# Gate products of a SwiGLU loop over 128 contraction rows in place of 96

## The chip, the cores and the metric

The kernel runs on one core of one Trainium2 chip. The metric is the device time of one execution in microseconds, the median of several runs. The five engines of the core are named PE (TensorE, matrix products), PEld (its loading of stationary operands), DVE (VectorE), ACT (ScalarE), POOL (GpSimd) and SP (SyncE, which here only issues transfers).

## What is computed

Three stages follow one another; the change touches the last.

```python
attn_out = _attn_ref(...)            # Fourier layer over 8 x 3072 tokens of width 256
x = attn_out.reshape(B * S, D)
x = _moe_ref(x=x, **moe_kwargs)      # ends in  c @ slot_out   (c: softmax over 32 slots)
# _moe2_ref:
g = x @ w_gate                       # 256 -> 1536
silu = g * (1.0 / (1.0 + np.exp(-g)))
val = x @ w_val
return (silu * val @ w_out)          # 1536 -> 256
```

Since x = c @ slot_out, the kernel computes slot_out @ w_gate and slot_out @ w_val once (32 x 1536 each, called the gates below) and then, for every token, c times these 32 rows.

## The kernel before

The first 600 us of the program are the Fourier layer, the logits, and the softmax statistics over all 24,576 tokens. The change lies behind that, in the function after_slots, which computes the 32 slot outputs and then runs the loop.

Numbers are held as a high part and a low part in a type (F32R) that TensorE multiplies in one pass. The softmax c of each token block stands in DRAM in the scratch array c_scr, index 0 the high part and index 1 the low part. A product of two split numbers is written as one matrix product whose contraction rows are blocks of 32: the stationary tile gst holds gate blocks, the moving tile cst holds softmax blocks, and row block r of the one meets row block r of the other. Before the change there are three blocks, so 96 rows: high x high, high x low, low x high.

- gates(t) computes a third of the gates into PSUM (tile pq), 64 rows for each of gate and value, in which the 32 slots stand twice. gate_high(c, m) copies 64 rows to gst rows 0 to 63 (the high part twice); gate_low(c, m) writes PSUM minus high part. There are eight such pairs (four column pieces c, two matrices m). They run ahead of and during the first steps of the loop.
- load_c(b, q) fills one cst tile by transfers that POOL's queue issues, one per block of 32 rows and 128 KB each. There are 24 tiles (8 batches b, 3 pieces q); a tag has two buffers.
- The loop has 576 steps (8 batches x 3 pieces x 2 halves x 12 column blocks of the gates). In a step gv(i) issues two gate products, L1561 into pg and L1562 into pv, with 512 moving columns. ACT forms sg = silu(pg) (L1564), DVE forms h = sg * pv (L1566). Then split(i-1) makes hh on ACT (L1573) and hl on DVE (L1574), and mm_out(i-3) issues six products with 128 rows (L1586) into the output accumulators o. So a step has eight products of TensorE, two of which have 96 rows.
- rest_c(b+1) interleaves the making of the next batch's softmax with the steps of batch b. POOL multiplies (L1622) and subtracts (L1636), SP stores both parts to c_scr, and then POOL's queue issues the transfers of the three load_c of the next batch (written at steps 50, 54 and 58 of the batch), and the load of the batch after that (L1612).

Order on an engine is the order in which the code is written. Each transfer of POOL's queue takes the next of eight semaphores in a ring, shown below as DMASW0 to DMASW7, and waits for the transfer that had this semaphore before it.

Of the kernel before, what the change touches and what calls it, by code (L numbers as in the profile page):

```python
# [10 lines left out]
F32 = mybir.dt.float32  # L11
F32R = mybir.dt.float32r
# [10 lines left out]
R1 = 96  # L23
# [340 lines left out]
def kernel(  # L364
# [49 lines left out]
    def open_pool(name, side="left", bufs=1, **k):  # L414
        cm = tc.tile_pool(name=name, bufs=bufs, reuse_waits="tile", **({} if "space" in k else {"side": side}), **k)
        pool = cm.__enter__()
        open_pools[name] = cm
        return pool
# [990 lines left out]
    def after_slots(ypool, chp):  # L1409
# [17 lines left out]
        for k in range(2):  # L1427
            nc.tensor.matmul(
                out=pst[:, k], lhsT=acc[:, k * 128:(k + 1) * 128], rhs=fd[:, 0:32], start=True, stop=True
# [51 lines left out]
        wp = open_pool("wp")  # L1481
        wp.tile([128, 312], F32, name="pad0", bufs=1)
        cp = open_pool("p2c", bufs=2)
        cuts = ((0, 0, 128), (0, 128, 512), (1, 0, 512), (2, 0, 512))
        gst = {(c, m): wp.tile([R1, cuts[c][2] - cuts[c][1]], F32R, name=f"gst{c}{m}") for c in range(4) for m in range(2)}

        def gate_cols(m, f):
            c, k = ((0, 0), (1, f - 1), (2, f - 4), (3, f - 8))[(f > 0) + (f > 3) + (f > 7)]
# [11 lines left out]
        cst_t = {}  # L1500

        def load_c(b, q):
            cst_t[b, q] = t = cp.tile([R1, 1024], F32R, tag=f"cst{q}", name="cst")
            for r, s in ((0, 0), (1, 1), (2, 0)):
                nc.gpsimd.dma_start(out=t[32 * r:32 * r + 32], in_=c_scr[b, s, 32 * q:32 * q + 32])

        load_c(0, 0)
        load_wo(wp, 0)
        load_wg(wp, "wg", 1, 2)
# [15 lines left out]
        ps = open_pool("p2ps", bufs=2, space=PSUM)  # L1525
        load_wo(hp, 1)
        load_c(0, 1)
        load_wo(hp, 2)
        load_c(0, 2)

        pq = {}
# [14 lines left out]
        def gate_low(c, m):  # L1546
            t, a, e = cuts[c]
            nc.vector.tensor_sub(  # L1548
                out=gst[c, m][64:96], in0=pq[t][64 * m:64 * m + 32, a:e], in1=gst[c, m][0:32].bitcast(F32)
            )  # L1550

        h_t, hs_t, po_t, ob_t = {}, {}, {}, {}
# [101 lines left out]
        for i in range(n + 3):  # L1654
            b, at = divmod(i, per)
            if at == 0:
                jobs = rest_c(b + 1) if b + 1 < B else {}
            if i == 0:
                gates(0)
                gates(1)  # L1660
            for c, m in {
                0: ((0, 0), (0, 1), (1, 0), (1, 1)), 1: ((2, 0),), 2: ((2, 1),), 4: ((3, 0),), 5: ((3, 1),),
            }.get(i, ()):
                gate_high(c, m)
                gate_low(c, m)
            if i < n:
                gv(i)
            if i == 1:
                gates(2)
            if 1 <= i <= n:  # L1670
                split(i - 1)
            for job in jobs.get(at, ()):
                job()
            if i >= 3:
                mm_out(i - 3)
        hp.tile([128, 504], F32, name="pad1", bufs=1)

    with tc.manual_schedule():
        after_slots(*phase1())
        for name in ("p2ps", "p2h", "p2c", "wp", "ypool", "chp"):  # L1680
            close_pool(name)
# [31 lines left out]
```

## Time and profile before

| | |
|---|---|
| median of 3 runs | 1684.48 us (1683.44 to 1685.2) |
| profiled execution, its own time | 1683.11 us |
| span of its trace | 1681.3 us |
| first gate product of the loop starts at | 604.76 us |
| PE busy | 1658.4 us (99%) |
| DVE busy | 1296.7 us (77%) |
| ACT busy | 981.4 us (58%) |
| POOL busy | 306.5 us (18%) |

The rows come from one profiled execution; times count from the start of its span. A matmul's record has a modelled end and overlaps the next one, so what a product costs in a dense stream is the distance between starts, not the duration shown.

### The profile page before, as it was taken

Reading aid. Unit: us, or ns where it says so; the run is one execution under the profiler, and the core shown is the slowest. Engines: PE = TensorE matmul, PEld = TensorE weight load, DVE = VectorE, ACT = ScalarE, POOL = GpSimd, SP = SyncE. Lnnn points to the kernel's source line nnn. Section 1 sums busy time; section 2 is a strip of 40 time slices with the busy share of each in tenths; the row PEclk is TensorE's granted clock in tenths of the full one; section 3 lists DMA queues with packets and bytes.
Section 4 is the critical chain, followed back from the end, with each engine's and each line's share of the span. In section 5 each row is a group of like instructions: output and inputs, shape, how many; then the busy total and the mean of one; then the engine's idle time right before and its main releaser. Section 6 shows DMA issues by size and latency. Waiting matters only on the chain.

```text
span 1681.3 us, 23324 instructions
## 1 busy us (share of the span) xinstructions
PE 1658.4 (99%) x8186; PEld 1282.1 (76%) x8186; DVE 1296.7 (77%) x2205; ACT 981.4 (58%) x1832; POOL 306.5 (18%) x353
## 2 busy tenths in 40 slices
PE   7999999999999999999999999999999999999998
PEld 4677676776767668888888888888888888888886
DVE  4789888888888558778778777778777777877776
ACT  2655565655656356656656656656655665665664
POOL 1334334334343421100100200200110110110000
PEclk9999999999999999999999999999999999999999
DMA  9356454546547971311300201311120031021111
GB/s 194 86 130 152 111 136 113 147 114 155 147 113 223 326 182 26 82 26 26 82 26 19 76 26 26 82 26 26 45 63 19 20 82 26 25 73 26 26 26 25
DMA packets 260164, 139.94 MB, mean 83 GB/s; under 512 B 210352, under 2 KB 243856, under 8 KB 260048
## 3 DMA queue, kind: packets, MB, share of 16 engines
q1 hardware_dynamic: 249648, 116.57, 26.7%
q0 software_dynamic: 9344, 21.63, 5.0%
q8 instruction: 65, 1.06, 0.3%
q14 instruction: 51, 0.42, 0.1%
q10 hardware_dynamic: 1056, 0.26, 0.1%
HBM read 72.74 MB, written 40.50 MB: 67 GB/s over the span
## 4 chain that ended last, share of the span: by engine, by line
PE 91%; DVE 3%; DMA 2%; ACT 1%; SPq 1%; issue 1%; POOL 0%; DVEq 0%; ACTq 0%; POOLq 0%
PE o L1586 47%; PE pb L701 10%; PE pv L1562 8%; PE pg L1561 8%; PE ac L587 6%; PE ac L613 4%; PE ch L1056 1%; PE ch L1104 1%; PE ch L798 1%; SPq L827 1%; PE ch L866 1%; DMA x<-in_x_dram 1%; PE ch L1012 1%; PE ch L926 1%; DVE xg L632 1%
## 5 line engine op out<-in xcount | busy, mean ns | idle before, releaser
L1586 PE MATMUL o<-hh,wo 128*128 128x512 f32 x2304 | 718.0, 393 | 0.0
L1564 ACT ACTIVATE sg<-pg 128x512 f32<-128x512 f32 x576 | 345.6, 600 | 410.7 <-PE pg L1561 410.6
L1566 DVE TENSOR_TENSOR h<-sg,pv 128x512 f32<-128x512 f32 x576 | 393.3, 683 | 245.3 <-ACT sg L1564 243.7
L1586 PEld LDWEIGHTS o<-hh,wo 128*128 128x128 f32 x2304 | 433.9, 188 | 104.3
L1586 PE MATMUL o<-hl,wo 128*128 128x512 f32 x1152 | 454.0, 394 | 0.0
L1574 DVE TENSOR_TENSOR hl<-h,hh 128x512 fp32r<-128x512 f32 x576 | 397.2, 690 | 0.1
L1573 ACT ACTIVATE hh<-h 128x512 fp32r<-128x512 f32 x576 | 358.9, 623 | 0.3 <-DVE h L1566 0.2
L1586 PEld LDWEIGHTS o<-hl,wo 128*128 128x128 f32 x1152 | 216.0, 188 | 47.1
L1562 PE MATMUL pv<-cst,gst 96*128 96x512 f32 x576 | 228.9, 397 | 0.6 <-DVE gst L1548 0.6
L1561 PE MATMUL pg<-cst,gst 96*128 96x512 f32 x576 | 227.5, 395 | 0.0
L701 PE MATMUL pb<-xg,whl 128*128 128x512 f32 x576 | 177.1, 437 | 0.3 <-DVE yt L756 0.2
L701 PEld LDWEIGHTS pb<-xg,whl 128*128 128x128 f32 x576 | 104.4, 189 | 44.2 <-issue 22.5
L1562 PEld LDWEIGHTS pv<-cst,gst 96*128 96x128 f32 x576 | 109.4, 190 | 25.8 <-DVE gst L1548 0.9
L1561 PEld LDWEIGHTS pg<-cst,gst 96*128 96x128 f32 x576 | 108.2, 188 | 25.4 <-DVE gst L1548 1.3
L772 POOL TENSOR_TENSOR yt<-r,yt 128x512 f32<-128x512 f32 x75 | 97.5, 1301 | 160.9 <-ACT yt L763 110.6
L592 DVE STREAM_TRANSPOSE chan<-ac 128x512 f32<-128x512 f32 x128 | 89.9, 707 | 37.3 <-PE ac L587 33.0
L1622 POOL TENSOR_TENSOR e<-e,rs 96x256 f32<-96x256 f32 x28 | 22.6, 835 | 502.4 <-DVE rs L1619 502.4
L587 PE MATMUL ac<-xq,fwd 96*128 96x512 f32 x224 | 111.6, 604 | 1.2 <-DVE xg L632 0.8
L613 PEld LDWEIGHTS ac<-cm,chan 128*128 128x128 f32 x768 | 101.0, 196 | 15.1 <-issue 6.6
L613 PE MATMUL ac<-cm,chan 128*128 128x128 f32 x768 | 105.0, 283 | 1.1 <-DVE xg L632 1.1
L701 PE MATMUL pb<-sg,whl 128*128 128x512 f32 x288 | 87.2, 426 | 0.3 <-POOL sg L651 0.3
L651 POOL TENSOR_TENSOR sg<-sf,sg 128x256 fp32r<-128x256 f32 x75 | 56.5, 758 | 119.5 <-ACT sg L647 104.1
(157 smaller groups left out, 1459.3 us busy)
## 6 DMA issues: line engine op xcount, KB each, us to landing
out_dram<-ob SPq DMA_DIRECT2D x190, 128.0 KB, 2.2
yi<-yt SPq DMA_DIRECT2D x368, 64.0 KB, 2.1
xq<-in_x_dram SPq DMA_DIRECT2D x28, 768.0 KB, 6.3
cst<-c_scr POOLq DMA_DIRECT2D x72, 128.0 KB, 2.9
w2s<-in_moe_w_dram SPq DMA_DIRECT2D x7, 1024.0 KB, 10.4
x<-in_x_dram SPq DMA_DIRECT2D x4, 768.0 KB, 10.6
cv<-in_moe_w_gate_dram SPq DMA_DIRECT2D x6, 512.0 KB, 4.7
w_scr<-cv SPq DMA_DIRECT2D x12, 256.0 KB, 2.2
```

Of the source, the lines that this page charges most:

```text
L587: nc.tensor.matmul(out=pt, lhsT=fwd[:, 8 - 8 * dh:136 - 8 * dh], rhs=T[kq][:, :, d1:d1 + 16], start=True, stop=True)
L592: nc.vector.transpose(out=chan[:, 12 * dh:12 * dh + 16, d0:d0 + 16, :].rearrange("p j d i -> p d j i"), in_=T[ka].rearrange("p n d -> p d n"),
L613: nc.tensor.matmul(out=pt[:, :, q:q + 2, i // 2, :], lhsT=chan[:, 16 * dh + j // 2, :, j % 2], rhs=cm[:, j, :].rearrange("p (c h k) -> p c ...
L701: nc.tensor.matmul(out=pt, lhsT=w[:, dh, m, es], rhs=xx, start=m != 1 and dh == 0 and n == 0, stop=dh == 1 and n == 2, skip_group_check=True,)
L772: e.tensor_sub(out=part(), in0=quarters(T[kr]), in1=part())
L1561: nc.tensor.matmul(out=pg, lhsT=gate_cols(0, f), rhs=rhs, start=True, stop=True)
L1562: nc.tensor.matmul(out=pv, lhsT=gate_cols(1, f), rhs=rhs, start=True, stop=True)
L1564: nc.scalar.activation(out=sg, in_=pg, func=AF.Silu)
L1566: nc.vector.tensor_mul(out=h, in0=sg, in1=pv)
L1573: nc.scalar.activation(out=hh, in_=h, func=AF.Copy)
L1574: nc.vector.tensor_sub(out=hl, in0=h, in1=hh.bitcast(F32))
L1586: nc.tensor.matmul(out=po_t[0][k], lhsT=w[:, f % 4, k * 128:(k + 1) * 128], rhs=a, start=(f == 0 and m == 0), stop=(f == NF - 1 and m == 2 ...
```

## The change

A fourth block is added: the low part of the gates times the low part of the softmax. The tile gst and the tile cst get 128 rows, gate_low writes 64 rows in place of 32 (the low part twice), and load_c issues four transfers in place of three, the fourth again from the low part of c_scr. No product, no load of a stationary operand and no instruction of ACT, DVE or SP is added.

```diff
-        gst = {(c, m): wp.tile([R1, cuts[c][2] - cuts[c][1]], F32R, name=f"gst{c}{m}") for c in range(4) for m in range(2)}
+        gst = {(c, m): wp.tile([128, cuts[c][2] - cuts[c][1]], F32R, name=f"gst{c}{m}") for c in range(4) for m in range(2)}
...
         def load_c(b, q):
-            cst_t[b, q] = t = cp.tile([R1, 1024], F32R, tag=f"cst{q}", name="cst")
-            for r, s in ((0, 0), (1, 1), (2, 0)):
+            cst_t[b, q] = t = cp.tile([128, 1024], F32R, tag=f"cst{q}", name="cst")
+            for r, s in ((0, 0), (1, 1), (2, 0), (3, 1)):
                 nc.gpsimd.dma_start(out=t[32 * r:32 * r + 32], in_=c_scr[b, s, 32 * q:32 * q + 32])
...
         def gate_low(c, m):
             t, a, e = cuts[c]
             nc.vector.tensor_sub(
-                out=gst[c, m][64:96], in0=pq[t][64 * m:64 * m + 32, a:e], in1=gst[c, m][0:32].bitcast(F32)
+                out=gst[c, m][64:128], in0=pq[t][64 * m:64 * m + 64, a:e], in1=gst[c, m][0:64].bitcast(F32)
             )
```

The order of PE, ACT, DVE and SP stays as it was; POOL's has 24 more transfers (337 rows against 313). The first place is POOL's queue just ahead of the loop: the three load_c of batch 0 between the loads of the output weights (wo). Before:

```order
L1505 DMA cst<-c_scr 32x1024 [waits DMASW1_49,PE_49]
L1505 DMA cst<-c_scr 32x1024 [waits DMASW2_49]
L1505 DMA cst<-c_scr 32x1024 [waits DMASW3_49]
L1496 DMA wo_5497<-w_scr_61 128x4x256 [waits DMASW4_49]
L1496 DMA wo_5499<-w_scr_62 128x4x256 [waits DMASW5_49]
L1496 DMA wo_5592<-w_scr_61 128x4x256 [waits DMAHW0_49,DMAHW3_49,DMASW6_49,DMAHW6_49,DMASW0_49,PE_49]
L1496 DMA wo_5594<-w_scr_62 128x4x256 [waits DMASW7_49]
```

The same place in the changed kernel:

```order
L1505 DMA cst<-c_scr 32x1024 [waits DMASW1_49,PE_49]
L1505 DMA cst<-c_scr 32x1024 [waits DMASW2_49]
L1505 DMA cst<-c_scr 32x1024 [waits DMASW3_49]
L1505 DMA cst<-c_scr 32x1024 [waits DMASW4_49]
L1496 DMA wo_5498<-w_scr_61 128x4x256 [waits DMASW5_49]
L1496 DMA wo_5500<-w_scr_62 128x4x256 [waits DMASW6_49]
L1496 DMA wo_5593<-w_scr_61 128x4x256 [waits DMAHW0_49,DMAHW3_49,DMASW7_49,DMAHW6_49,DMASW0_49,PE_49]
L1496 DMA wo_5595<-w_scr_62 128x4x256
```

A fourth transfer of the first tile stands ahead of the weights, and every later transfer has moved on in the ring. The second place is POOL's queue in batch 0, where the three tiles of batch 1 are fetched. Before:

```order
L1636 TENSOR_TENSOR clo<-ct,chi 96x256 [waits Activation_49] x3
L1505 DMA cst<-c_scr 32x1024 [waits DMAHW3_49,DMASW1_49]
L1505 DMA cst<-c_scr 32x1024 [waits DMAHW4_49,DMASW2_49]
L1505 DMA cst<-c_scr 32x1024 [waits DMASW3_49]
L1505 DMA cst<-c_scr 32x1024 [waits DMASW4_49]
L1505 DMA cst<-c_scr 32x1024 [waits DMASW5_49]
L1505 DMA cst<-c_scr 32x1024 [waits DMASW6_49]
L1505 DMA cst<-c_scr 32x1024 [waits DMASW7_49]
L1505 DMA cst<-c_scr 32x1024
L1505 DMA cst<-c_scr 32x1024 [waits DMASW1_49]
L1612 DMA e<-e_scr 96x1024 [waits DMASW2_49,Pool_49]
```

The same place in the changed kernel:

```order
L1505 DMA cst<-c_scr 32x1024 [waits DMAHW4_49,DMASW5_49]
L1505 DMA cst<-c_scr 32x1024 [waits DMASW6_49]
L1505 DMA cst<-c_scr 32x1024 [waits DMASW7_49]
L1505 DMA cst<-c_scr 32x1024 [waits DMASW0_49]
L1505 DMA cst<-c_scr 32x1024 [waits DMASW1_49]
L1505 DMA cst<-c_scr 32x1024 [waits DMASW2_49]
L1505 DMA cst<-c_scr 32x1024
L1505 DMA cst<-c_scr 32x1024 [waits DMASW4_49]
L1505 DMA cst<-c_scr 32x1024 [waits DMASW5_49]
L1505 DMA cst<-c_scr 32x1024 [waits DMASW6_49]
L1505 DMA cst<-c_scr 32x1024 [waits DMASW7_49]
L1612 DMA e<-e_scr 96x1024 [waits DMASW0_49,Pool_49]
```

Twelve transfers (one more, with DMAHW3 and DMASW4, stands ahead of these) have taken the place of nine, and the last four of them wait for transfers of the same burst.

## Rows read from the trace of the kernel before

**Rows 1.** The page: busy time by engine, and the granted clock in 40 slices.

```profile
PE 1658.4 (99%) x8186; PEld 1282.1 (76%) x8186; DVE 1296.7 (77%) x2205; ACT 981.4 (58%) x1832; POOL 306.5 (18%) x353
...
PEclk9999999999999999999999999999999999999999
```

**Rows 2.** The page: shares of the chain of work that ended last, by line.

```profile
PE o L1586 47%; PE pb L701 10%; PE pv L1562 8%; PE pg L1561 8%; PE ac L587 6%; PE ac L613 4%; PE ch L1056 1%; PE ch L1104 1%; PE ch L798 1%; SPq L827 1%; PE ch L866 1%; DMA x<-in_x_dram 1%; PE ch L1012 1%; PE ch L926 1%; DVE xg L632 1%
```

**Rows 3.** The page's costliest groups: busy, mean ns of one, idle before and its releaser.

```profile
L1586 PE MATMUL o<-hh,wo 128*128 128x512 f32 x2304 | 718.0, 393 | 0.0
...
L1566 DVE TENSOR_TENSOR h<-sg,pv 128x512 f32<-128x512 f32 x576 | 393.3, 683 | 245.3 <-ACT sg L1564 243.7
L1586 PEld LDWEIGHTS o<-hh,wo 128*128 128x128 f32 x2304 | 433.9, 188 | 104.3
...
L1561 PE MATMUL pg<-cst,gst 96*128 96x512 f32 x576 | 227.5, 395 | 0.0
...
L1561 PEld LDWEIGHTS pg<-cst,gst 96*128 96x128 f32 x576 | 108.2, 188 | 25.4 <-DVE gst L1548 1.3
```

**Rows 4.** Timeline of PE, one step: start, duration in us, operation.

```profile
1000.31 0.39 PE L1586 MATMUL o<-hl,wo 128*128 128x512 f32 x1
1000.53 0.40 PE L1561 MATMUL pg<-cst,gst 96*128 96x512 f32 x1
1000.76 0.40 PE L1562 MATMUL pv<-cst,gst 96*128 96x512 f32 x1
1001.00 0.63 PE L1586 MATMUL o<-hh,wo 128*128 128x512 f32 x2
...
1002.39 0.39 PE L1561 MATMUL pg<-cst,gst 96*128 96x512 f32 x1
```

**Rows 5.** Timeline of PE, end of the loop.

```profile
1667.73 0.40 PE L1561 MATMUL pg<-cst,gst 96*128 96x512 f32 x1
...
1671.44 0.61 PE L1586 MATMUL o<-hh,wo 128*128 128x512 f32 x2
...
1674.84 0.61 PE L1586 MATMUL o<-hh,wo 128*128 128x512 f32 x2
```

**Rows 6.** Timeline of PE in the Fourier stage, a run of products with 128 rows.

```profile
249.31 2.26 PE L701 MATMUL pb<-sg,whl 128*128 128x512 f32 x9
```

**Rows 7.** Timeline ahead of the loop: POOL's issues, the gates, the first steps.

```profile
593.20 1.52 POOL L1505 DMA_DIRECT2D cst<-c_scr  x3 [11.59 <-PE ph L1443]
594.70 1.54 POOL L1496 DMA_DIRECT2D wo<-w_scr  x2
...
603.47 0.28 DVE L1548 TENSOR_TENSOR gst<-pq,gst 32x128 fp32r<-32x128 f32 x1 [2.34 <-ACT gst L1544]
...
604.24 0.60 PE L1537 MATMUL pq<-wg,tail 128*64 128x512 f32 x2
604.76 0.50 PE L1561 MATMUL pg<-cst,gst 96*128 96x512 f32 x1
...
604.93 0.55 DVE L1548 TENSOR_TENSOR gst<-pq,gst 32x384 fp32r<-32x384 f32 x1 [0.55 <-ACT gst L1544]
```

**Rows 8.** Groups by line and shape, 600 to 1600 us: gate_low with 512 columns.

```profile
L1548 DVE TENSOR_TENSOR gst<-pq,gst 32x512 fp32r<-32x512 f32 x4 | 2.7, 685 | 0.1
```

**Rows 9.** Transfers of cst, us from issue to landing: one issued by 594.7, then all.

```profile
cst<-c_scr POOLq DMA_DIRECT2D x1, 128.0 KB, 6.3
...
DMA to landing us min/median/max: 2.4/2.9/9.6
```

**Rows 10.** Groups by line, 685.11 to 689 us: POOL's burst, DVE beside it.

```profile
L1505 POOL DMA_DIRECT2D cst<-c_scr x8 | 3.9, 501 | 0.7 <-DMA c_scr<-clo 0.7
...
L1574 DVE TENSOR_TENSOR hl<-h,hh 128x512 fp32r<-128x512 f32 x3 | 2.1, 685 | 0.0
```

**Rows 11.** Timeline of PE around that burst, first and last gate product.

```profile
683.62 0.39 PE L1561 MATMUL pg<-cst,gst 96*128 96x512 f32 x1
...
689.17 0.40 PE L1561 MATMUL pg<-cst,gst 96*128 96x512 f32 x1
```

## The prediction

> **What bounds the kernel now.** I read the page first. PE is busy 99% of the span and its granted clock shows 9 in all 40 slices, so the upper of its two levels (2.4 GHz) throughout [rows 1]. The chain of work that ended last goes the same way: the loop's eight products per step, L1586, L1562 and L1561, hold 47 + 8 + 8 = 63% of it, and no transfer of cst and no subtraction of gate_low is among its larger shares [rows 2]. The groups say why nothing else matters in the loop: the products there sat idle for 0.0 us, while DVE waited 245.3 us for ACT ahead of h, that is 0.43 us in each of 576 steps [rows 3]. So DVE has slack in every step, and only what changes the distance between the starts of two products, or what makes PE wait at the loop's entry, can move the end.
>
> The durations of products (393 to 395 ns) overlap, so I took distances from the timeline of PE. From the gate product at 1000.53 us to the one at 1667.73 us are 360 steps: 667.20 / 360 = 1.853 us a step, or 0.232 us a product [rows 4, 5]. 576 such steps are 1067 us. Within a step, three distances touch a product with 96 rows: into pg, pg to pv, and pv to the first of the six. They take 1001.00 - 1000.31 = 0.69 us, 0.230 each. The six distances from there to the next pg take 1002.39 - 1001.00 = 1.39 us, 0.232 each, and five of the six lie between products with 128 rows [rows 4]. The reader is to see that 96 rows buy no time now.
>
> **The change, part by part.**
>
> *Gate products, 96 to 128 rows (1152 of them).* If time went with rows, two products a step would take a third longer: 2 x 0.23 / 3 = 0.153 us, 88 us over 576 steps. The rows exclude it: a product has 512 moving columns either way, its record is 395 ns with 96 rows and 393 ns with 128, and its distance is 0.230 against 0.232 [rows 3, 4]. The load of the stationary operand takes 188 ns with 96 rows and 188 ns with 128 [rows 3]. Value: 0. What a stream of only 128-row products takes, with ACT and DVE at work beside it, the trace shows in another stage: nine products in a row at L701 take 2.26 us, so (2.26 - 0.40) / 8 = 0.2325 us each, with 0.40 us for the last one's record [rows 6]. The bounds: below, the end of the loop, where only L1586 runs and ACT and DVE fall silent, shows (1674.84 - 1671.44) / 15 = 0.2267 us [rows 5]. Three distances at 0.2267 are 0.680 in place of 0.690 us, so -0.010 x 576 = -5.8 us. Above, the longest distance in the step shown, 0.24 us from pv to the first of the six, for all three: 0.72 in place of 0.69, +0.03 x 576 = +17 us. I take 0 because the nearest rows, the six products of the same step and L701, both stand at 0.232.
>
> *gate_low, 32 to 64 rows (8 subtractions).* Four stand one behind another ahead of the first steps and take 0.28 us (two with 128 columns) and 0.55 us (two with 384) [rows 7]. The same kind of operation takes 685 ns on 32 rows with 512 columns and 683 ns on 128 rows with 512 columns [rows 8, 3]: rows cost nothing. Value 0; if they doubled, 2 x 0.28 + 2 x 0.55 = +1.7 us on the entry, with the other four under DVE's slack.
>
> *The fourth transfer, at the entry.* The first tile's three are issued from 593.20 to 594.72 us, so the fourth goes out at about 594.7 and pushes two weight loads by 0.5 us. The first gate product starts at 604.76 us, and behind a gates product that PE issued at 604.24: PE was still busy there, it did not wait for cst [rows 7]. The transfer issued last of the three landed 6.3 us after its issue; the same delay puts the fourth at 601.0 us, and the longest delay of all 72 transfers, 9.6 us, at 604.3 us, still ahead of 604.76 [rows 9]. Value 0. The cover is 0.4 us in the worst case and 3.7 us in the usual one.
>
> *The 21 others.* In each later batch POOL issues a burst, about 0.50 us an issue [rows 10]. It grows from 9 + 1 to 12 + 1 issues, about 5.0 to 6.5 us. Queued behind the added issues is only the load for the batch after (L1612), whose data DVE first reads at step 8 of the next batch, over 30 steps later. The last four wait, by the ring of semaphores, for the first four of the same burst, issued 4.0 us before; a usual landing is 2.9 us [rows 9]. The tile is due at step 72 of the batch. The product at 683.62 us, just before the burst, is (1667.73 - 683.62) / 1.853 = 531 steps ahead of step 574, so it is step 43, and 29 steps or 53.7 us are left: far more than 6.5 + 9.6 us. Does the burst itself slow anything? During it DVE's subtraction of hl, which has both inputs in SBUF, takes 685 ns against 683 for h over the whole kernel, and PE makes three steps in 689.17 - 683.62 = 5.55 us, 1.85 each, as everywhere [rows 10, 11, 3]. Value 0. The bound on the other side: if a burst's three added issues held DVE for all their 1.5 us within one step, 1.5 - 0.43 = 1.1 us of it would pass the slack, and seven bursts would cost 7.5 us; ten such issues that cost nothing today speak against any of it.
>
> The sum is 0 against the profiled execution's 1683.11 us (span 1681.3 us, 1.8 us around it). That execution lies 1.4 us, or 0.08%, below the median of the three runs, 1684.48 us, which spread from 1683.44 to 1685.2. The forecast for the median is therefore 1684.5 us.
>
> **The rivals.**
>
> *Slower: the fourth strip of 32 rows costs the loads their cover.* Today a gate product leaves the last 32 rows of the array unused, and the load of the next operand might profit. After the change no product does. Its place is the three distances of each step, and the limit is three bare loads, 3 x 0.188 x 576 = 325 us; with the 0.24 us above it is +17 us, 1702 us. It decides from 3.4 us (0.2%) on, which is 3.4 / 1152 = 3 ns a gate product. Against it: five of the six distances between 128-row products hide a 188 ns load each and stand at 0.232 us [rows 3, 4], and L701's at 0.2325 us [rows 6]. Chance 0.05.
>
> The Trainium skill speaks for this rival: its page "TensorE: Matmul & The Clock Gate", Part 3, The mechanism, says that the load of weights overlaps a running matmul only when the two use different groups of 32 rows. By that rule the six 128-row products of a step would each show load and product one behind the other; the trace does not agree, with 0.232 us between starts beside a load of 0.188 us, since less than 0.05 us is left for a product's own columns.
>
> *Faster: going from 96 to 128 rows and back costs something now.* Uniform products would then run as at the loop's end: -5.8 us, 1678.7 us. For it: 0.2267 us is real for 128-row products alone. Against it: L701 has one shape too and stands at 0.2325 us, and inside the step, distances between equal shapes are no shorter (0.232) than those that touch a change (0.230), so the loop's end is more likely fast because ACT and DVE are silent. Chance 0.06.
>
> *Slower at the entry: the first tile's fourth block lands late.* To cost 3.4 us it would have to land at 608.2 us, 13.5 us after its issue, against 9.6 us for the longest seen. It would give some 1688 us. Chance 0.02.
>
> *The change does nothing.* PE's sequence of instructions is the same and only its active rows differ, which is just what the forecast says costs nothing; this gives the same time.
>
> **How the numbers follow.** A difference of 0.2%, 3.4 us, is about what a measurement of this kernel can tell from no change. The forecast, no change, has 0.87 and covers 1681.1 to 1687.9, with the +1.7 us of gate_low inside it; faster has 0.06, slower 0.05 + 0.02 = 0.07. The range 1681 to 1688 us holds the first case alone and leaves out about 0.13, so it need not reach to the others.
>
> **What would show it.** In the changed kernel's profile the gate products should read 128x512 with records near 395 ns and loads at 188 ns; gate products should stand 1.853 us apart in the steady loop; gate_low should stay at 0.28, 0.55 and 0.68 us; the first gate product should start within 0.5 us of 604.76 us, released by PE or DVE and not by a transfer; POOL should show 96 transfers of cst at about 0.5 us. I am wrong if the step's length moves by 6 ns or more (576 x 6 ns = 3.4 us), or if the loop's first product waits for cst.

## The result and the profile after

The changed kernel takes 1661.52 us (median of four runs, 1660.82 to 1662.99), the kernel before 1684.84 us beside it: 23.3 us less, ratio 0.9858 with a 95% interval of 0.9837 to 0.9878. I had forecast no change, 1681 to 1688 us.

The page of the changed kernel, to be held against [rows 1] and [rows 3] (busy us, mean ns of one, idle before and its releaser):

```profile
PE 1636.2 (99%) x8186; PEld 1279.8 (77%) x8186; DVE 1295.8 (78%) x2205; ACT 981.2 (59%) x1832; POOL 317.6 (19%) x377
...
PEclk9999999999999999999999999999999999999999
...
L1586 PE MATMUL o<-hh,wo 128*128 128x512 f32 x2304 | 709.3, 389 | 0.0
...
L1566 DVE TENSOR_TENSOR h<-sg,pv 128x512 f32<-128x512 f32 x576 | 393.6, 683 | 224.6 <-ACT sg L1564 224.4
...
L1561 PE MATMUL pg<-cst,gst 128*128 128x512 f32 x576 | 224.4, 390 | 0.0
...
L1561 PEld LDWEIGHTS pg<-cst,gst 128*128 128x128 f32 x576 | 108.3, 188 | 24.6 <-DVE gst L1548 1.3
```

Nothing was taken away from any engine: the same number of products, the same loads at 188 ns, the same work on DVE. PE is still busy 99%, only for 22 us less, and the granted clock is the same. DVE's wait ahead of h fell from 245.3 to 224.6 us, so DVE had the slack to follow. What became shorter is the distance between starts. The timeline of PE, one step of the changed kernel and a gate product near the end (start, duration, operation), to be held against [rows 4]:

```profile
999.77 0.39 PE L1586 MATMUL o<-hl,wo 128*128 128x512 f32 x1
1000.00 0.39 PE L1561 MATMUL pg<-cst,gst 128*128 128x512 f32 x1
1000.23 0.39 PE L1562 MATMUL pv<-cst,gst 128*128 128x512 f32 x1
1000.45 0.61 PE L1586 MATMUL o<-hh,wo 128*128 128x512 f32 x2
1000.91 0.39 PE L1586 MATMUL o<-hl,wo 128*128 128x512 f32 x1
1001.13 0.61 PE L1586 MATMUL o<-hh,wo 128*128 128x512 f32 x2
1001.59 0.39 PE L1586 MATMUL o<-hl,wo 128*128 128x512 f32 x1
1001.81 0.39 PE L1561 MATMUL pg<-cst,gst 128*128 128x512 f32 x1
...
1647.36 0.39 PE L1561 MATMUL pg<-cst,gst 128*128 128x512 f32 x1
```

From 1000.00 to 1647.36 us are 357 steps, 1.8133 us each, against 1.8533 before: 0.040 us a step, times 576 is 23.0 us, the whole gain. All eight distances have become 0.2267 us, also the five between output products, which the edit does not touch. That is the distance that [rows 5] shows at the loop's end.

The transfers went as forecast. The first gate product starts at 605.35 us, 0.59 later than before, a little more than the 0.5 us that I had allowed; but POOL's first issue of cst already starts 0.58 later than in [rows 7], behind a product of the stage ahead: the shift comes from ahead of the change. The timeline ahead of the loop:

```profile
593.78 2.02 POOL L1505 DMA_DIRECT2D cst<-c_scr  x4 [11.59 <-PE ph L1443]
...
601.77 3.65 PE L1537 MATMUL pq<-wg,tail 128*64 128x512 f32 x16 [0.39 <-DVE tail L1520]
...
604.05 0.28 DVE L1548 TENSOR_TENSOR gst<-pq,gst 64x128 fp32r<-64x128 f32 x1 [2.34 <-ACT gst L1544]
...
605.35 0.50 PE L1561 MATMUL pg<-cst,gst 128*128 128x512 f32 x1
```

The subtraction on 64 rows takes the 0.28 us it took on 32. The transfers of cst (issues, then us to landing), and POOL's burst of batch 0:

```profile
cst<-c_scr POOLq DMA_DIRECT2D x96, 128.0 KB, 3.3
...
DMA to landing us min/median/max: 2.4/3.3/8.3
```

```profile
684.35 5.37 POOL L1505 DMA_DIRECT2D cst<-c_scr  x11 [0.68 <-DMA c_scr<-clo]
```

The median transfer lands after 3.3 us, against 2.9 before, and no product waits for it. Eleven of the burst's twelve issues take 5.37 us, 0.49 each; the steps beside them take 1.813 to 1.814 us, like all others.

### The profile page after: what moved, and what is told of

Its sections match the earlier page's. It is cut to its first block, busy times and chain, and to the rows that moved or that the text cites. A ratio compares the mean times of both kernels' runs of the same rounds, so it can differ in the third digit from the quotient of the medians.

```text
span 1659.0 us, 23348 instructions
## 1 busy us (share of the span) xinstructions
PE 1636.2 (99%) x8186; PEld 1279.8 (77%) x8186; DVE 1295.8 (78%) x2205; ACT 981.2 (59%) x1832; POOL 317.6 (19%) x377
## 4 chain that ended last, share of the span: by engine, by line
PE 91%; DVE 4%; DMA 2%; ACT 1%; issue 1%; SPq 1%; POOL 0%; DVEq 0%; ACTq 0%; POOLq 0%
PE o L1586 47%; PE pb L701 10%; PE pv L1562 8%; PE pg L1561 8%; PE ac L587 7%; PE ac L613 4%; PE ch L1056 1%; PE ch L1104 1%; PE ch L798 1%; PE ch L866 1%; PE ch L1012 1%; PE ch L926 1%; DVE xg L632 1%; SPq L827 1%; DVE sf L638 0%
## 5 line engine op out<-in xcount | busy, mean ns | idle before, releaser
L1586 PE MATMUL o<-hh,wo 128*128 128x512 f32 x2304 | 709.3, 389 | 0.0
L1566 DVE TENSOR_TENSOR h<-sg,pv 128x512 f32<-128x512 f32 x576 | 393.6, 683 | 224.6 <-ACT sg L1564 224.4
L1586 PE MATMUL o<-hl,wo 128*128 128x512 f32 x1152 | 448.1, 389 | 0.0
L1562 PE MATMUL pv<-cst,gst 128*128 128x512 f32 x576 | 224.2, 389 | 0.6 <-DVE gst L1548 0.6
L1561 PE MATMUL pg<-cst,gst 128*128 128x512 f32 x576 | 224.4, 390 | 0.0
L701 PE MATMUL pb<-xg,whl 128*128 128x512 f32 x576 | 177.1, 437 | 0.4 <-DVE yt L756 0.2
L701 PEld LDWEIGHTS pb<-xg,whl 128*128 128x128 f32 x576 | 104.4, 189 | 44.2 <-issue 22.7
L1561 PEld LDWEIGHTS pg<-cst,gst 128*128 128x128 f32 x576 | 108.3, 188 | 24.6 <-DVE gst L1548 1.3
L1562 PEld LDWEIGHTS pv<-cst,gst 128*128 128x128 f32 x576 | 108.0, 188 | 23.1 <-DVE gst L1548 0.9
L587 PE MATMUL ac<-xq,fwd 96*128 96x512 f32 x224 | 111.6, 604 | 1.1 <-DVE xg L632 0.8
L701 PE MATMUL pb<-sg,whl 128*128 128x512 f32 x288 | 87.2, 426 | 0.3 <-POOL sg L651 0.3
```

The lines of the kernel that those rows point to most:

```text
L587: nc.tensor.matmul(out=pt, lhsT=fwd[:, 8 - 8 * dh:136 - 8 * dh], rhs=T[kq][:, :, d1:d1 + 16], start=True, stop=True)
L701: nc.tensor.matmul(out=pt, lhsT=w[:, dh, m, es], rhs=xx, start=m != 1 and dh == 0 and n == 0, stop=dh == 1 and n == 2, skip_group_check=True,)
L1561: nc.tensor.matmul(out=pg, lhsT=gate_cols(0, f), rhs=rhs, start=True, stop=True)
L1562: nc.tensor.matmul(out=pv, lhsT=gate_cols(1, f), rhs=rhs, start=True, stop=True)
L1566: nc.vector.tensor_mul(out=h, in0=sg, in1=pv)
L1586: nc.tensor.matmul(out=po_t[0][k], lhsT=w[:, f % 4, k * 128:(k + 1) * 128], rhs=a, start=(f == 0 and m == 0), stop=(f == NF - 1 and m == 2 ...
```

## The experiments

The theory after the result: what cost time before was not 96 rows, but going from products of 128 rows to products of 96 and back in one stream, twice in each step. The rivals: 96-row products themselves slow the stream; or the rows have nothing to do with it, and the transfers, the tiles or the data have.

The distances in the table below are mean ns between starts, worked out from the starts of some 550 steps of each trace (272 pairs of steps for the paired order), in the order of the stream. Each trace is of one execution.

```text
                  rows of the products       distances, the stream's order           step us
before            96 96 then 6 x 128         233 235 234 233 233 225 229 231          1.8533
after             8 x 128                    227 in every place                       1.8133
e1 96 restored    96 96 then 6 x 128         233 235 234 233 233 225 229 231          1.8533
e2 one of two     128 96 then 6 x 128        227 233 237 233 231 227 227 227          1.8400
e3 all 96         8 x 96                     227 in every place                       1.8133
e4 apart          (96 then 3 x 128) twice    233 238 233 231, twice                   1.8667
e5 paired         4 x 96 then 12 x 128       233 236 228 233 234 233 231, then 227    1.8333
e6 gates over 64  64 64 then 6 x 128         335 322 337 236 228 233 231 318          2.2400
e7 (slowest run)  128 then 7 x 96            238 236 240 229 233 236 224 231          1.8667
e10 all 64        8 x 64                     227 in every place                       1.8133
```

**e1: only the products' rows put back.**

```diff
-            nc.tensor.matmul(out=pg, lhsT=gate_cols(0, f), rhs=rhs, start=True, stop=True)
-            nc.tensor.matmul(out=pv, lhsT=gate_cols(1, f), rhs=rhs, start=True, stop=True)
+            nc.tensor.matmul(out=pg, lhsT=gate_cols(0, f)[0:96], rhs=rhs[0:96], start=True, stop=True)
+            nc.tensor.matmul(out=pv, lhsT=gate_cols(1, f)[0:96], rhs=rhs[0:96], start=True, stop=True)
```

> The changed kernel with the 128-row tiles, the four transfers and the 64-row subtractions, but the two gate products run over rows 0 to 95 alone (the fourth block is left out of the result). If the rows of the products made the gain, by a change of shape in the stream or by 96 rows themselves, the step is 1.853 us again and the time 1685 us. If the gain came with the transfers, the tiles or their place, 1661 us.

1684.4 us, ratio to before 0.9999 (0.999 to 1.0009), and the distances of before, place by place. With all 96 transfers and the 128-row tiles in place the gain is gone: it lies in the rows of the products alone. The edit cuts the load of the stationary operand to 96 rows together with the product; which of the two carries the price, no run here separates.

**e2: one of the two gate products over 96 rows** (the changed kernel, with pv alone cut as in e1).

> The changed kernel with pg over 128 rows and pv over 96 (the value branch leaves out the fourth block). Theory of change: what costs is going from 128 to 96 rows and back, about 20 ns each time; both changes are still there in each step, so 1.853 us a step and 1685 us. Theory of 96 rows: each 96-row product costs the stream 20 ns, one of two is left, 1.833 us a step and 1673 us.

1676.73 us, ratio 0.9951 (0.9936 to 0.9966): between the two. The timeline of PE shows one step:

```profile
1000.52 0.39 PE L1561 MATMUL pg<-cst,gst 128*128 128x512 f32 x1
1000.75 0.40 PE L1562 MATMUL pv<-cst,gst 96*128 96x512 f32 x1
1000.98 0.63 PE L1586 MATMUL o<-hh,wo 128*128 128x512 f32 x2
1001.45 0.39 PE L1586 MATMUL o<-hl,wo 128*128 128x512 f32 x1
1001.68 0.62 PE L1586 MATMUL o<-hh,wo 128*128 128x512 f32 x2
1002.14 0.39 PE L1586 MATMUL o<-hl,wo 128*128 128x512 f32 x1
1002.36 0.39 PE L1561 MATMUL pg<-cst,gst 128*128 128x512 f32 x1
```

The table has the finer reading: the four distances from pv on are 6, 11, 6 and 4 ns over 226.7, together 26.7 ns, and then the stream is back at 226.7. One 96-row product lengthens distances up to three products behind it, among products of one shape. Neither theory had that size: 13.3 ns less than the pair of before, not 40 and not 20.

**e3: all eight products over 96 rows.**

```diff
-                        out=po_t[0][k], lhsT=w[:, f % 4, k * 128:(k + 1) * 128], rhs=a,
+                        out=po_t[0][k], lhsT=w[0:96, f % 4, k * 128:(k + 1) * 128], rhs=a[0:96],
```

> The kernel before with the six output products over rows 0 to 95 too, so that all eight products of a step have 96 rows (a quarter of the contraction of the output products is left out of the result). Theory of change: no change of shape is left in the loop, 1.813 us a step and 1661 us. Theory of 96 rows: eight such products cost 8 x 20 ns a step, 1.973 us, about 1754 us.

1661.61 us, ratio 0.9862 (0.9846 to 0.9879). This is the run that parts the theories: eight 96-row products a step are as fast as eight of 128, to the ns (page of e3):

```profile
L1586 PE MATMUL o<-hh,wo 96*128 96x512 f32 x2304 | 709.3, 389 | 0.0
...
L1561 PE MATMUL pg<-cst,gst 96*128 96x512 f32 x576 | 224.4, 390 | 0.0
```

**e4: the two gate products apart.** On PE: pg, three output products, pv, three output products.

```diff
             if i < n:
                 gv(i)
+            if i >= 3:
+                mm_out(i - 3, 0)
+            if i < n:
+                gv2(i)
...
-                mm_out(i - 3)
+                mm_out(i - 3, 1)
```

> The kernel before with another order on TensorE: pg, three output products, pv, three output products, so four changes of shape a step in place of two, with the same products. Theory of change: 4 x 20 ns over 1.813, 1.893 us a step and 1708 us. Theory of 96 rows: 1.853 us a step and 1685 us, as before, since there are still two such products.

1691.75 us, ratio 1.0041 (1.0026 to 1.0056): slower, as the theory of change has it and that of 96 rows does not, but by 7 us and not by 23. The step is 53.3 ns over 1.8133, which is twice the 26.7 ns of e2, with the same four lengthened distances after each 96-row product (233, 238, 233 and 231 ns, to within half a ns): two spells (runs of 96-row products in a row) of one product each. The price per change that I had put at 20 ns does not hold for a lone product.

**e5: two steps taken together**, four 96-row products in a row and then twelve of 128.

```diff
-            if i >= 3:
-                mm_out(i - 3)
+            late = [j for j in (i - 4, i - 3) if j >= 0] if i % 2 else [i - 3] if i == n + 2 else []
+            for j in late:
+                mm_out(j)
```

> The kernel before with two steps taken together on TensorE: four gate products of 96 rows in a row, then twelve output products, so half as many changes of shape. Theory of a fixed price per spell of 96-row products (40 ns for the two in a row of before): 20 ns a step over 1.813, 1.833 us and 1673 us. Theory of a price per spell plus one per 96-row product (13.3 ns each, fitted to 26.7 ns for a spell of one and 40 ns for a spell of two): 5 x 13.3 = 67 ns for two steps, 1.847 us a step and 1681 us. Theory of 96-row products alone: 1685 us.

1674.03 us, ratio 0.9934 (0.9919 to 0.9949). Two steps take 3.6667 us, 40 ns over the uniform stream, the same 40 ns as for a spell of two before. So a spell of four costs what a spell of two costs. The formula with a part per product, which I had fitted to e2 and before, is out.

**e6: gate products over 64 rows** (before, with both products cut to rows 0 to 63).

> The kernel before with the gate products over rows 0 to 63 (the low part of the gates is left out of the result). If any change of the number of rows costs the same, 1.853 us a step and 1685 us. If the price goes with the strips of 32 rows that come and go, two in place of one, 80 ns over 1.813, 1.893 us a step and 1708 us.

1904.84 us, ratio 1.1305 (1.1286 to 1.1325), far outside both. A step takes 2.240 us, 0.427 over the uniform stream, 0.213 on average for each of its two changes. The timeline of the loads shows where it goes (start, duration, and the idle time before):

```profile
1000.90 0.19 PEld L1586 LDWEIGHTS o<-hl,wo 128*128 128x128 f32 x1
1001.44 0.18 PEld L1561 LDWEIGHTS pg<-cst,gst 64*128 64x128 f32 x1 [0.36 <-issue]
1001.55 0.19 PEld L1562 LDWEIGHTS pv<-cst,gst 64*128 64x128 f32 x1
1002.10 0.19 PEld L1586 LDWEIGHTS o<-hh,wo 128*128 128x128 f32 x1 [0.36 <-issue]
```

At both changes, and only there, the load does not start with the running product; it comes 0.36 us after the load before it has ended. In the kernel before, the load of pg starts beside the output product that [rows 4] shows at 1000.31 us:

```profile
1000.31 0.19 PEld L1561 LDWEIGHTS pg<-cst,gst 96*128 96x128 f32 x1
```

Between 96 and 128 rows the loads keep their cover, and what is lost is small. Why a change to 64 rows loses the cover and one to 96 does not, no run here shows.

**e7: the stream turned round**, seven products over 96 rows and pg alone over 128 (e3 with the changed kernel's pg).

> The stream turned round: seven products of a step over 96 rows and pg alone over 128 (a quarter of the contraction of the output products and the fourth block of the value branch are left out of the result). If the price is that of a change, there are two a step again, 27 to 40 ns over 1.813, 1677 to 1685 us. If it is per spell plus per 96-row product, 8 x 13.3 = 107 ns, 1.920 us a step and 1723 us.

1677.9 us, ratio 0.9977 (0.9951 to 1.0004). The ten runs lie apart, eight from 1675.57 to 1681.12 us and two at 1692.57 and 1694.28; the trace is of the one at 1694.28 and shows 53.3 ns a step over 1.8133, while the median's time stands for (1677.9 - 1661.5) / 576 = 28 ns. Both are far from the 107 ns of a price per 96-row product, so the price is that of a change again. It varies from execution to execution, from about 27 to 53 ns; what decides, these runs don't show, and of the shorter ones there is no trace.

**e8: zeros in the fourth block of the gates.**

```diff
-                out=gst[c, m][64:128], in0=pq[t][64 * m:64 * m + 64, a:e], in1=gst[c, m][0:64].bitcast(F32)
+                out=gst[c, m][64:96], in0=pq[t][64 * m:64 * m + 32, a:e], in1=gst[c, m][0:32].bitcast(F32)
             )
+            g = gst[c, m][0:32].bitcast(F32)
+            nc.vector.tensor_sub(out=gst[c, m][96:128], in0=g, in1=g)
```

> The changed kernel with 128 rows in each product, but zeros in the fourth block of the gates (made by eight more subtractions of 0.3 to 0.7 us ahead of and in the first steps, up to 2 us on the entry; the fourth block adds nothing to the result). If the number of rows addressed decides, 1.813 us a step and 1661 to 1664 us. If what the rows hold decides, a step longer than 1.813 us, up to 1685 us.

1663.8 us, ratio 0.9876 (0.9861 to 0.9892), 1.8133 us a step. The 2.3 us over the changed kernel lie in the loop's first steps, where the second step's pg now waits for DVE's subtractions and its pv does again (in the changed kernel only the pv waits, 0.62 us):

```profile
608.99 0.47 PE L1563 MATMUL pg<-cst,gst 128*128 128x512 f32 x1 [0.71 <-DVE gst L1552]
610.14 0.47 PE L1564 MATMUL pv<-cst,gst 128*128 128x512 f32 x1 [0.68 <-DVE gst L1552]
```

By the traces' starts the first 20 steps take 38.26 us, against 35.61 in the changed kernel, and all later ones together the same 1006.4. The number of rows decides, not what stands in the gates' rows: padding them with zeros would have done the same.

**e9: the same idea in the Fourier stage.**

```diff
-    ones = keep.tile([32, R1], F32, name="ones")
+    ones = keep.tile([128, R1], F32, name="ones")
...
-                d = sb(chp, dg, [32, 32], "dg")
-                nc.vector.tensor_scalar_mul(d, ident[0:32, 0:32], new[0:32])
+                d = sb(chp, dg, [128, 32], "dg")
+                nc.vector.tensor_scalar_mul(d, ident[:, 0:32], new)
...
-                        out=pt, lhsT=spi[0:32, c, :], rhs=T[kq][0:32, c, 0, :], start=(c == 0), stop=(c == 1)
+                        out=pt, lhsT=spi[:, c, :], rhs=T[kq][:, c, 0, :], start=(c == 0), stop=(c == 1)
...
-                            out=pt[0:32, c, :, 0], lhsT=spf[0:64, c, :], rhs=T[t2][0:64, half[h], 24],
+                            out=pt[0:32, c, :, 0], lhsT=spf[:, c, :], rhs=T[t2][:, half[h], 24],
```

> The changed kernel with three small products of the Fourier stage padded from 64, 32 and 32 rows to 128 rows of which the added ones meet zeros (the result is the same). In that stage 64 neighbours in TensorE's order go between products of up to 64 rows and products of more. If such a change there costs the 213 ns that two of them a step cost in the loop over 64 rows, 64 x 0.213 = 13.6 us are to be had where TensorE is on the chain: 1648 us. If these places wait for other engines anyway, 1661 us.

1659.25 us, ratio 0.9854 (0.9839 to 0.9869) against 0.9858 (0.9837 to 0.9878) for the changed kernel: not to be told apart, and the 13.6 us are not there. In the traces' starts only L976 (the product of ones and dg, 96 stationary columns) answers: the median from a product of L587 to it falls from 522 to 429 ns, and from it to L701 from 174 to 84 ns, at four places each; the distances next to all 16 such products shrink by 1.4 us together. The products with 64 and 32 stationary columns (L904, L1062) keep theirs (256 ns from L1056 to L1062 in both). That their number of columns, which differs from their neighbours' too, holds the price up is what I think; it was not tried.

**e10: all eight products over 64 rows** (e3 with 64).

> The kernel before with all eight products of a step over rows 0 to 63 (a third of the gate products' contraction and half of the output products' is left out of the result). If the 427 ns a step of the loop over 64 rows are the price of its two changes, 1.813 us a step and 1661 us. If 64-row products are slow by themselves, more than 1905 us.

1659.73 us, ratio 0.9858 (0.9841 to 0.9874); the page of e10:

```profile
L1586 PE MATMUL o<-hh,wo 64*128 64x512 f32 x2304 | 705.8, 386 | 0.0
...
L1561 PE MATMUL pg<-cst,gst 64*128 64x512 f32 x576 | 222.6, 386 | 0.0
```

A uniform stream runs at 226.7 ns at 64, 96 and 128 rows. The 427 ns of e6 are the price of its changes alone.

**e11: the order of weights that L701 has**, because its 0.2325 us had misled me.

```diff
-                for m, (a, w) in enumerate(((hh, woh), (hh, wol), (hl, woh))):
+                for m, (a, w) in enumerate(((hh, woh), (hl, woh), (hh, wol))):
```

> The changed kernel with the three output products of an accumulator in the order of the Fourier stage's L701: high weights twice in a row, then the low weights (same products, same result). L701 stands at 0.2325 us a product with 128 rows throughout. If loading the same weights twice in a row is what makes L701 longer, the loop's products go to about 0.232 us, 1.86 us a step and 1685 us. If it is something else in that stage, 1.813 us a step and 1661 us.

1662.17 us, ratio 0.9866 (0.9849 to 0.9883), 1.8133 us a step. Loading the same weights twice running costs nothing here. Why L701 stands at 0.2325 us with 128 rows throughout stays open.

## Why the prediction was wrong

**The step that failed** is the sum's first term: gate products at 0, where -23 us was measured, "because the nearest rows, the six products of the same step and L701, both stand at 0.232". I took the five distances between 128-row products [rows 4] as what such a stream costs by itself. They were not clean: the 96-row products ahead of them had lengthened them, as e2 shows with three lengthened distances among products of 128 rows alone. So "distances between equal shapes are no shorter (0.232) than those that touch a change (0.230)" was no test at all, and it came from a single step read to 0.01 us: over the steps that the table averages, the three that touch a 96-row product average 232.9 ns and the other five 230.9. The second witness, L701 [rows 6], has nearly the same mean for another reason that these runs don't name: by the trace's starts the distances of that run go 230, 232 and 238 ns over and over, which no row of the table does. The third row I had, the loop's end at 0.2267 us [rows 5], was the right one; I put its lower value down to ACT and DVE falling silent. The trace of before has rows against that:

```profile
1671.26 1.48 DVE L1574 TENSOR_TENSOR hl<-h,hh 128x512 fp32r<-128x512 f32 x2
1671.38 0.63 ACT L1573 ACTIVATE hh<-h 128x512 fp32r<-128x512 f32 x1 [0.24 <-DVE h L1566]
...
1671.44 0.61 PE L1586 MATMUL o<-hh,wo 128*128 128x512 f32 x2
...
1672.80 0.61 PE L1586 MATMUL o<-hh,wo 128*128 128x512 f32 x2
```

From 1671.44 to 1672.80 us are six distances, 0.2267 us each, with DVE at work until 1672.74 and ACT until 1672.01. And in the changed kernel ACT and DVE are as busy as ever, and the distance is 0.2267 in every place.

**The faster rival had the mechanism, and its price and chance were wrong.** "Going from 96 to 128 rows and back costs something now" is what e1, e3, e4 and e5 show. I priced it on the three distances that touch a change: -5.8 us. Taken on all eight, with the same 0.2267 us of [rows 5], it is (0.2317 - 0.2267) x 8 x 576 = -23 us, the measured one; so the term was mis-sized by a factor of four, and a chance of 0.06 rested on the unclean rows.

**Right:** rows cost nothing by themselves (e3 and e10: 0.2267 us at 64, 96 and 128). gate_low takes as long on 64 rows as on 32. The fourth transfers are hidden: e1 has them all and takes 1684.4 us. DVE had its slack.

**The slower rival** (the loads lose their cover when no strip is free) went the wrong way round. The Trainium skill's page "TensorE: Matmul & The Clock Gate", Part 3, The mechanism, has the load overlap a running product only if the two use different groups of rows, in its list of what overlaps (the paragraph ahead of that list names a second case, a load into a background buffer of weights). These traces disagree with the list: with 128 rows in both, load and product overlap fully (227 ns between starts, a load of 188), and the cover is lost where the number of rows changes between 64 and 128 (e6).

## What to carry to other kernels

In a stream of dense products that bounds a kernel, look at the number of contraction rows of neighbours before the number of products: a stream with one shape was fastest whether it had 64, 96 or 128 rows, and padding a 96-row product to 128, with the low part or with zeros, cost the stream nothing. Where shapes must differ, keep the odd ones together: four 96-row products in a row cost what two did. Above all keep 64-row products out of a 128-row stream. All of this was measured with F32R products of 512 moving columns. And to price a dense stream, take the distance between starts from a stretch where nothing else is mixed in: a neighbour's cost shows up products later, on innocent rows.

## What was not expected of the hardware

- A uniform stream of 512-column products keeps 226.7 ns between starts to within 1 ns, in every place of the step, at 64, 96 and 128 rows.
- One 96-row product in a 128-row stream costs 26.7 ns, spread over four distances (6, 11, 6, 4 ns); spells of two and of four cost 40 ns. Before the change the step's sum alternated between 1.845 and 1.862 us, and e7 shows 53.3 ns in its trace and about 27 by the times of most executions. The averages 26.7, 40 and 53.3 are whole multiples of 13.3 ns; the rule behind them stays open.
- A change between 128 and 64 rows costs 213 ns, against 13 to 20 ns for one between 128 and 96 (27 in e7's trace), and is seen as a load that no longer starts beside the running product.
